# 384-token feed-forward steps, a 32x32 convolution and a new instruction order in a fused linear-attention and gated-feed-forward kernel

## The chip, the cores and the metric

The kernel runs on one core of a Trainium2 chip. The metric is the device time of one execution in microseconds (us), lower is better: the median of three runs. A profile of one execution stands beside it. Its span is a little shorter than the time of the run that it belongs to.

Five engines work side by side, each in the order of its own instructions: TensorE (PE), VectorE (DVE), ScalarE (ACT), GpSimd (POOL) and SyncE (SP), which here only issues transfers. Matrix products land in PSUM, in banks; all else lies in SBUF.

## The reference

A linear attention with a decaying state feeds a gated feed-forward block. B = 4 batches, H = 8 heads, S = 768 tokens, D = 48, all float32; H*D = 384 channels.

```python
def _attn_ref(r, k, v, w, u):
    for t in range(S):
        cur = einsum('bhd,bhe->bhde', u[None] * kt, vt)
        y[:, :, t] = einsum('bhd,bhde->bhe', rt, state + cur)
        state = w[None, :, :, None] * state + einsum('bhd,bhe->bhde', kt, vt)

def _moe_ref(x, w_val, conv_w, w_out):            # x: y as [B, S, 384]
    xp = np.concatenate([zeros((B, K - 1, D)), x], axis=1)     # K = 5 taps, causal
    for k in range(K):
        gate_pre += conv_w[k][None, None, :] * xp[:, k:k + S, :]
    gate = 1.0 / (1.0 + np.exp(-gate_pre))
    return gate * (x @ w_val) @ w_out
```

## The kernel before

The attention works in 12 units n of 256 tokens (three to a batch), each of two chunks cl of 128. The order of all instructions is a long list of short names (ORDER), which the kernel walks; every engine gets its instructions in the order in which their names stand. The names that matter here: `r`, `k`, `v` loads; `RS`, `KS` scaling of r and k by powers of the decay; `RT`, `KT` their transposes on PE, `RE`, `KE` the copies of these out of PSUM; `PR`, `S`, `SE`, `DV` the bonus of the current token; `CV` the cast of v; `A`, `M` scores and their mask; `KV`, `ID`, `ZE` the state; `YD`, `Y`, `YE` the output of the attention, written to `xT` (channels on partitions, tokens along the row); `C` convolution, `SG` sigmoid, `V` values, `HT` gate times value, `O` projection, `OE` its copy, `st` the store. A star moves the step to another engine or queue.

```python
    ld = ctx.enter_context(tc.tile_pool(name="ld", bufs=7))        # k and v
    ldr = ctx.enter_context(tc.tile_pool(name="ldr", bufs=6))      # r
    outp = ctx.enter_context(tc.tile_pool(name="outp", bufs=11))   # outputs
    psum = ctx.enter_context(tc.tile_pool(name="psum", bufs=8, space=bass.MemoryType.PSUM))

    def load_kv(n, cl, nm, eng):          # 192 KB, rows of 48 floats
        eng.dma_start(out=d[n][:, cl], in_=src[b, :, t0 : t0 + C, :].transpose([1, 0, 2]))

    def carry(n, cl):                     # ID: add the carried state
        kv_ps = st["kv_ps", n, cl]
        nc.vector.tensor_tensor(out=kv_ps, in0=kv_ps, in1=st["zin", n, cl], op=ALU.add)

    def evac_k(n, cl=None):               # KE
                nc.scalar.copy(out=st["kT", n].rearrange(...)[:, cls[0] : cls[1]], in_=tr)
```

The feed-forward works on 256 tokens at a time. The five taps are products with 64x64 diagonal matrices (`cwd`). 384 channels are three groups of 128; the third group is laid beside the first two, so that each of two banks holds 256 + 128 columns:

```python
    def conv(n):
        g_ps = [bank([128, W + C]) for i in range(2)]          # W = 256, C = 128
        for T0, t1, tn in ((0, 0, W), (2, 0, 0)):
            for t in range(KW):
                for q in range(2):
                    for i in range(2):
                        T = 2 if T0 else i
                        c0, n0, o0 = (i * C, C, W) if T0 else (t1, tn, t1)
                        rows = slice(64 * q, 64 * q + 64)
                        qo = (q + i) % 2
                        nc.tensor.matmul(
                            out=g_ps[i][64 * qo : 64 * qo + 64, o0 : o0 + n0],
                            lhsT=cwd[rows, T, t, :],
                            rhs=xT[rows, T, t0 + c0 + t : t0 + c0 + t + n0],
                            ...)
    # values: three matmuls of 256 and three of 128 columns for each of two halves
    # projection: three matmuls of 384 columns for each chunk of 128 tokens
    # the last unit is done chunk by chunk in functions of its own (conv_l, value_l, project_l ...)
    def store(n):                          # one row of 384 floats (1536 B) after the other
        nc.sync.dma_start(
            out=out[b, cu * W : cu * W + W, :].rearrange("(c p) n -> p c n", p=128),
            in_=st["o", n])
```

In ORDER, all stores stand behind the last load on the queue of SP.

Of the kernel before, what the change touches and what calls it, by code (L numbers as in the profile page):

```python
# [16 lines left out]
def kernel(  # L17
# [15 lines left out]
    C = 128  # L33
# [12 lines left out]
    ld = ctx.enter_context(tc.tile_pool(name="ld", bufs=7))  # L46
    ldr = ctx.enter_context(tc.tile_pool(name="ldr", bufs=6))
# [3 lines left out]
    outp = ctx.enter_context(tc.tile_pool(name="outp", bufs=11))  # L51
# [54 lines left out]
    io_i32 = consts.tile([128, 1], mybir.dt.int32)  # L106
    nc.gpsimd.iota(io_i32, pattern=[[0, 1]], base=0, channel_multiplier=1)
    io_j = consts.tile([128, 2], mybir.dt.int32)
    nc.gpsimd.iota(io_j, pattern=[[1, 2]], base=0, channel_multiplier=2)
    mask = consts.tile([128, 128], BF16)  # L110
    make_upper_triangular(nc, mask, val=1.0, diag=False)

    io_f = consts.tile([128, 1], F32)
    nc.vector.tensor_copy(io_f, io_i32)
    sc_k = consts.tile([128, U], F32)
    for cl in range(U):
        nc.vector.tensor_scalar(
            sc_k[:, cl : cl + 1], io_f, scalar1=-1.0, scalar2=float(C - 1 - cl * C),
            op0=ALU.mult, op1=ALU.add,
        )  # L120
    sc_r = consts.tile([128, 2], F32)
    nc.vector.tensor_copy(sc_r, io_j)
    nc.vector.tensor_scalar_add(sc_r, sc_r, float(-C))
# [76 lines left out]
    nc.gpsimd.memset(wcm, 0.0)  # L200
    bdm = consts.tile([128, NP, 2, D], F32)
    nc.gpsimd.memset(bdm, 0.0)
    for par in range(2):
        nc.gpsimd.memset(bdm[64 * par : 64 * par + 64, :, par, :], 1.0)
# [3 lines left out]
    wv_st = consts.tile([128, NT, DM], F32)  # L208
    wo_st = consts.tile([128, NT, DM], F32)

    wval = consts.tile([128, NT, 4, 128], BF16)
    wout = consts.tile([128, 4, DM], BF16)
    cw5b = consts.tile([KW, DM], BF16)
    cwT = consts.tile([128, NT, KW], F32)
    cwd = consts.tile([128, NT, KW, 64], BF16)
    id64 = consts.tile([128, 64], BF16)

    for q in range(2):
        rows = slice(64 * q, 64 * q + 64)
        nc.vector.tensor_copy(id64[rows], ident[rows, rows])  # L220
# [11 lines left out]
    def cw_evac():  # L232
        nc.vector.tensor_copy(cwT, st["cw_ps"][:, :, 0:KW])

    def cw_diag():
        nc.vector.tensor_tensor(
            out=cwd.rearrange("p t k x -> p (t k) x"),
            in0=id64[:, None, :].to_broadcast([128, NT * KW, 64]),
            in1=cwT.rearrange("p t k -> p (t k)")[:, :, None].to_broadcast([128, NT * KW, 64]),
            op=ALU.mult,  # L240
        )

    def cast_wval():
        wv = wv_st.rearrange("p k (t x) -> p k t x", x=128)
        nc.gpsimd.tensor_copy(wval[:, :, 0::2, :], wv[:, :, 0::2, :])
        nc.gpsimd.tensor_copy(wval[:, :, 1::2, 64:128], wv[:, :, 1:3, 0:64])
        nc.gpsimd.tensor_copy(wval[:, :, 1::2, 0:64], wv[:, :, 1:3, 64:128])

    def cast_wout(part):
        if part:  # L250
            nc.scalar.copy(out=wout[64:128, 1::2, :], in_=wo_st[0:64, 1:3, :])
            nc.scalar.copy(out=wout[0:64, 1::2, :], in_=wo_st[64:128, 1:3, :])
        else:
            nc.gpsimd.tensor_copy(wout[:, 0::2, :], wo_st[:, 0::2, :])


# [39 lines left out]
    def cast_v(n):  # L296
        vb = vb_t[n % 4]
        nc.scalar.copy(  # L298
            out=vb[:, :, 16 : 16 + 64 * H].rearrange("p c (h x) -> p c h x", x=64)[:, :, :, 0:D],
            in_=v_st[n],  # L300
        )
# [17 lines left out]
    def evac_k(n, cl=None):  # L319
        for cls, tr in st["tr", n]:  # L320
            if cl is None or cl == cls[0]:
                nc.scalar.copy(  # L322
                    out=st["kT", n].rearrange("x n (c i) -> x c n i", c=U)[:, cls[0] : cls[1]],
                    in_=tr,
                )
# [83 lines left out]
    def carry(n, cl):  # L409
        kv_ps = st["kv_ps", n, cl]  # L410
        nc.vector.tensor_tensor(out=kv_ps, in0=kv_ps, in1=st["zin", n, cl], op=ALU.add)
# [55 lines left out]
    def evac_y(n, cl):  # L467
        b, cu = divmod(n, NU)
        t0 = PAD + cu * W + cl * C
        nc.scalar.copy(out=xT_t[b % 2][:, :, t0 : t0 + C], in_=st["y_ps", n, cl])  # L470


    def conv(n):
        b, cu = divmod(n, NU)
        xT, t0 = xT_t[b % 2], cu * W
        g_ps = [bank([128, W + C]) for i in range(2)]
        for T0, t1, tn in ((0, 0, W), (2, 0, 0)):
            for t in range(KW):
                for q in range(2):
                    for i in range(2):  # L480
                        T = 2 if T0 else i
                        c0, n0, o0 = (i * C, C, W) if T0 else (t1, tn, t1)
                        rows = slice(64 * q, 64 * q + 64)
                        qo = (q + i) % 2
                        nc.tensor.matmul(  # L485
                            out=g_ps[i][64 * qo : 64 * qo + 64, o0 : o0 + n0],
                            lhsT=cwd[rows, T, t, :],
                            rhs=xT[rows, T, t0 + c0 + t : t0 + c0 + t + n0],
                            start=(t == 0 and T0 == 0 and t1 == 0),
                            stop=(t == KW - 1),  # L490
                            skip_group_check=True,
                        )
        st["g_ps", n] = g_ps

    def gate_at(n, i):
        if ("gate", n) not in st:
            st["gate", n] = ffn.tile([128, 2, W + C], BF16, name="gate")
        nc.scalar.activation(out=st["gate", n][:, i], in_=st["g_ps", n][i], func=AF.Sigmoid)  # L498

    def value(n, i):  # L500
        b, cu = divmod(n, NU)
        xT, t0 = xT_t[b % 2], PAD + cu * W
        v_ps = bank()[:, 0 : W + C]
        for kt in range(NT):
            nc.tensor.matmul(  # L505
                out=v_ps[:, 0:W],
                lhsT=wval[:, kt, i, :],
                rhs=xT[:, kt, t0 : t0 + W],
                start=(kt == 0),
                stop=(kt == NT - 1),  # L510
                skip_group_check=True,
            )
        for kt in range(NT):
            nc.tensor.matmul(  # L514
                out=v_ps[:, W : W + C],
                lhsT=wval[:, kt, 2 + i, :],
                rhs=xT[:, kt, t0 + i * C : t0 + i * C + C],
                start=False,
                stop=(kt == NT - 1),
                skip_group_check=True,  # L520
            )
        st["v_ps", n, i] = v_ps

    def gated(n, i):
        if ("hT", n) not in st:
            st["hT", n] = ffn.tile([128, 2, W + C], BF16, name="hT")
        nc.vector.tensor_tensor(  # L527
            out=st["hT", n][:, i], in0=st["v_ps", n, i], in1=st["gate", n][:, i], op=ALU.mult
        )

    def project(n, cl):
        hT = st["hT", n]
        o_ps = bank()[:, 0:DM]
        parts = [(0, cl * C, 0), (1, cl * C, 1)]
        parts.insert(1 + cl, (cl, W, 2 + cl))
        for j, (i, c0, k) in enumerate(parts):
            nc.tensor.matmul(  # L537
                out=o_ps,
                lhsT=hT[:, i, c0 : c0 + C],
                rhs=wout[:, k, :],  # L540
                start=(j == 0),
                stop=(j == 2),
            )
        st["o_ps", n, cl] = o_ps

    def evac_o(n, cl):
        if ("o", n) not in st:
            st["o", n] = outp.tile([128, U, DM], F32, name="o_sb")
        nc.scalar.copy(out=st["o", n][:, cl, :], in_=st["o_ps", n, cl])  # L549

    def store(n):
        b, cu = divmod(n, NU)
        nc.sync.dma_start(
            out=out[b, cu * W : cu * W + W, :].rearrange("(c p) n -> p c n", p=128),
            in_=st["o", n],
        )

    HC = C // 2  # L560
    WL = C + HC

    def conv_l(n, cl):
        b, cu = divmod(n, NU)
        xT, t0 = xT_t[b % 2], cu * W + cl * C
        g_ps = [bank()[:, 0:WL] for i in range(2)]
        for T0 in (0, 2):
            for t in range(KW):
                for q in range(2):
                    for i in range(2):  # L570
                        T = 2 if T0 else i
                        c0, n0, o0 = (i * HC, HC, C) if T0 else (0, C, 0)
                        rows = slice(64 * q, 64 * q + 64)
                        qo = (q + i) % 2
                        nc.tensor.matmul(
                            out=g_ps[i][64 * qo : 64 * qo + 64, o0 : o0 + n0],
                            lhsT=cwd[rows, T, t, :],
# [254 lines left out]
```

## Time and profile before

| what | value |
|---|---|
| time, median of 3 (range) | 104.25 us (103.94 to 104.44) |
| span of the profiled run (its time) | 101.9 us (103.68) |
| PE, DVE, ACT, POOL busy | 84.5, 73.5, 72.7, 66.1 us |
| moved | 20.37 MB in 67505 packets, mean 200 GB/s |
| of these under 512 B | 63510 |
| convolution matmuls | 440, and 80 in the last unit |
| scores: DVE mask | 48 of 681 ns, 30.9 us |

How to read it. A busy time is the sum of an engine's instructions. Matmuls overlap one another, so PE's busy time counts latencies, and the cost of a block of matmuls is taken from the timeline or from the chain of waits, where a piece has a start and a length. The chain of waits follows the last instruction back to what released it, again and again; a piece "DMA v_st" is a load that something waited for, "SPq" is the issue of a transfer. A row of a group reads: line, engine, operation, what is written from what, shapes, count, then busy us and mean ns, then idle time ahead of it and what ended it. Windows give the busy time of each engine in a stretch of the span.

### The profile page before, as it was taken

What the parts mean: (1) busy time and instruction counts of PE and PEld (TensorE: products, weight loads), DVE (VectorE), ACT (ScalarE), POOL (GpSimd) and SP (SyncE); (2) the same over time, 40 slices, a digit from 0 to 9 for tenths busy, and PEclk for the clock granted to TensorE, in tenths of its full rate; (3) what the DMA queues carried; (4) which work ended last, traced back from release to release, by engine and by line L of the source; (5) the groups of instructions that cost most, each with busy time, mean ns of one, the idle gap of its engine ahead of it and who ended that gap; (6) DMA issues with size and microseconds to landing.
All of it is one profiled execution on the core that took longest, in us unless ns stands there. A gap on an engine that the chain in (4) does not pass through costs nothing.

```text
span 101.9 us, 4626 instructions
## 1 busy us (share of the span) xinstructions
PE 84.5 (83%) x2017; PEld 69.4 (68%) x2017; DVE 73.5 (72%) x145; ACT 72.7 (71%) x126; POOL 66.1 (65%) x67
## 2 busy tenths in 40 slices
PE   1413987998969799989999999988999999999900
PEld 1202766876858587978887887876888788778500
DVE  4057798999765685889989998489678898980500
ACT  5457574999294998887988939688979868538510
POOL 7928678969499884999775686798692571400000
PEclk9999999999999999999999999999999999999985
DMA  0999999999989998999999999798989894750660
GB/s 7 253 220 168 234 175 192 270 244 171 277 165 249 203 216 180 200 185 250 173 191 223 187 248 222 142 204 187 185 162 251 306 363 145 271 198 7 250 218 5
DMA packets 67505, 20.37 MB, mean 200 GB/s; under 512 B 63510, under 2 KB 67484, under 8 KB 67484
## 3 DMA queue, kind: packets, MB, share of 16 engines
q1 hardware_dynamic: 64428, 19.18, 85.0%
q10 hardware_dynamic: 3056, 0.89, 4.0%
q8 instruction: 16, 0.26, 1.1%
q14 instruction: 5, 0.04, 0.1%
HBM read 15.35 MB, written 4.72 MB: 197 GB/s over the span
## 4 chain that ended last, share of the span: by engine, by line
PE 28%; SPq 24%; DMA 18%; POOL 12%; ACT 8%; issue 5%; POOLq 0%
SPq L69 19%; DMA v_st<-in_v_dram 15%; POOL dv L358 7%; PE bank L537 6%; PE bank L485 5%; PE bank L441 4%; POOL ks L289 4%; SPq L76 4%; DMA r_st<-in_r_dram 3%; ACT xT L470 2%; PE bank L505 2%; PE bank L427 2%; ACT kT L322 2%; PE bank L399 1%; ACT rT L282 1%
## 5 line engine op out<-in xcount | busy, mean ns | idle before, releaser
L385 DVE TENSOR_TENSOR at<-bank,mask 128x512 bf16<-128x512 f32 x48 | 30.9, 681 | 3.4 <-PE bank L372 3.3
L260 POOL TENSOR_TENSOR rs<-r_st,dr 128x768 bf16<-128x768 f32 x11 | 20.0, 1821 | 7.5 <-DMA r_st<-in_r_dram 7.5
L289 POOL TENSOR_TENSOR ks<-k_st,dk 128x768 bf16<-128x768 f32 x10 | 18.2, 1822 | 8.1 <-DMA k_st<-in_k_dram 4.4
L358 POOL TENSOR_TENSOR dv<-v_st,s_sb 128x768 bf16<-128x768 f32 x12 | 17.7, 1476 | 4.4 <-DVE s_sb L355 2.9
L282 ACT COPY rT<-bank 128x1024 bf16<-128x1024 bf16 (+1 forms) x13 | 15.9, 1231 | 2.6 <-PE bank L274 2.6
L322 ACT COPY kT<-bank 128x1024 bf16<-128x1024 bf16 (+1 forms) x13 | 12.5, 959 | 4.7 <-DVE pr L331 1.7
L527 DVE TENSOR_TENSOR hT<-bank,gate 128x384 bf16<-128x384 f32 x22 | 11.8, 552 | 4.2 <-PE bank L514 2.5
L470 ACT CAST xT<-bank 128x384 bf16<-128x384 f32 x24 | 11.0, 493 | 3.5 <-PE bank L441 3.5
L537 PE MATMUL bank<-wout,hT 128*128 128x384 bf16 x66 | 13.4, 327 | 0.0
L298 ACT CAST vb<-v_st 128x768 bf16<-128x768 f32 x12 | 10.0, 836 | 4.1 <-DMA v_st<-in_v_dram 4.1
L485 PE MATMUL bank<-xT,cwd 64*64 64x128 bf16 (+1 forms) x440 | 11.5, 245 | 0.9 <-ACT xT L470 0.4
L498 ACT ACTIVATE gate<-bank 128x384 bf16<-128x384 f32 x22 | 10.0, 493 | 2.6 <-PE bank L485 2.4
L485 PEld LDWEIGHTS <-cwd 64*64 64x64 bf16 x440 | 9.9, 106 | 2.5 <-issue 1.5
L549 ACT COPY o_sb<-bank 128x384 f32<-128x384 f32 x22 | 10.7, 501 | 1.2 <-PE bank L537 1.2
L505 PE MATMUL bank<-xT,wval 128*128 128x256 bf16 x66 | 10.8, 273 | 0.1
L312 PE MATMUL bank<-ident,ks 128*128 128x128 bf16 x96 | 8.8, 242 | 1.8 <-DVE ks L289 1.8
L372 PE MATMUL bank<-rT,kT 48*128 48x128 bf16 x192 | 9.0, 232 | 1.0 <-ACT kT L322 0.7
L331 DVE TENSOR_TENSOR pr<-bank,rT 128x1024 bf16<-128x1024 bf16 (+1 forms) x13 | 8.4, 645 | 1.9 <-ACT kT L322 1.3
L274 PE MATMUL bank<-ident,rs 128*128 128x128 bf16 x96 | 8.6, 242 | 1.1 <-DVE rs L260 0.8
L441 PE MATMUL bank<-at,vb 128*32 128x128 bf16 x384 | 9.0, 219 | 0.0
L312 PEld LDWEIGHTS <-ks 128*128 128x128 bf16 x96 | 6.8, 109 | 2.5 <-POOL rs L260 2.0
L274 PEld LDWEIGHTS <-rs 128*128 128x128 bf16 x96 | 6.7, 109 | 1.9 <-issue 1.0
(80 smaller groups left out, 137.8 us busy)
## 6 DMA issues: line engine op xcount, KB each, us to landing
k_st<-in_k_dram SPq DMA_DIRECT2D x24, 192.0 KB, 5.5
v_st<-in_v_dram SPq DMA_DIRECT2D x24, 192.0 KB, 4.5
out_dram<-o_sb SPq DMA_DIRECT2D x11, 384.0 KB, 4.5
r_st<-in_r_dram SPq DMA_DIRECT2D x9, 384.0 KB, 5.6
r_st<-in_r_dram ACTq DMA_DIRECT2D x2, 384.0 KB, 5.1
wv_st<-in_moe_w_val_dram SPq DMA_DIRECT2D x1, 576.0 KB, 6.2
wo_st<-in_moe_w_out_dram SPq DMA_DIRECT2D x1, 576.0 KB, 6.0
r_st<-in_r_dram SPq DMA_DIRECT2D x2, 192.0 KB, 3.5
```

Source lines behind the costliest of these rows:

```text
L69: eng.dma_start(out=d[n][:, cl], in_=src[b, :, t0 : t0 + C, :].transpose([1, 0, 2]))
L260: eng.tensor_tensor(out=rs_t[n % 2][:, :, ps[0] : ps[1], :, 0:D].rearrange("p s n a d -> p (n a) s d"), in0=r_st[n][:, hs], in1=dr[:, hs], ...
L274: nc.tensor.transpose(tr[:, s, p, :], rs_t[n % 2][:, s, ps[0] + p].rearrange("p a x -> p (a x)"), ident,)
L282: nc.scalar.copy(out=st["rT", n][:, ps[0] : ps[1], :].rearrange("x n (i s) -> x s n i", s=2), in_=st["r_tr", n, ps[0]],)
L289: eng.tensor_tensor(out=ks_t[n % 3][:, cs, :, :, 0:D].rearrange("p c n a d -> p c (n a) d"), in0=k_st[n][:, cs], in1=dk[:, cs], op=ALU.mult,)
L312: nc.tensor.transpose(tr[:, c, p, :], ks[:, cls[0] + c, p].rearrange("p a x -> p (a x)"), ident,)
L322: nc.scalar.copy(out=st["kT", n].rearrange("x n (c i) -> x c n i", c=U)[:, cls[0] : cls[1]], in_=tr,)
L358: eng.tensor_tensor(out=dv_t[n % 2].rearrange("p c (h d) -> p (c h) d", d=D), in0=v_st[n].rearrange("p c h d -> p (c h) d"), in1=st["s", n ...
L385: nc.vector.tensor_tensor(out=st["at", n, cl][:, par], in0=st["at_ps", n, cl][par], in1=mask[:, None, :].to_broadcast([128, NP, 128]), op= ...
L441: nc.tensor.matmul(out=y_ps[32 * q : 32 * q + 32, T, :], lhsT=lt, rhs=rh, start=False, stop=last, skip_group_check=True,)
L485: nc.tensor.matmul(out=g_ps[i][64 * qo : 64 * qo + 64, o0 : o0 + n0], lhsT=cwd[rows, T, t, :], rhs=xT[rows, T, t0 + c0 + t : t0 + c0 + t + ...
L537: nc.tensor.matmul(out=o_ps, lhsT=hT[:, i, c0 : c0 + C], rhs=wout[:, k, :], start=(j == 0), stop=(j == 2),)
```

## The change

It changes the feed-forward and, around it, the order of everything.

- The feed-forward works in steps of 384 tokens (half a batch), the last half batch in steps of 256 and 128. There are nine steps. Each of the three channel groups has a bank of its own.
- The convolution uses 32x32 diagonal matrices: 12 matmuls for each tap, each in a tile of its own of the PE array. The 64-column diagonals shrink to 32 columns. The channels come out rotated by 32 for the second and 64 for the third group, so the columns of w_val and the rows of w_out are rotated too (w_out while it is loaded, in five pieces).
- The stores write three token rows one after the other from each partition.
- The carried state is added by PE, with an identity matrix.
- Some copies out of PSUM move from ACT to DVE, three casts of v to POOL, two scalings of r to DVE.
- Seven early loads have their issue on the queue of ACT, where there were two. Buffers for k and v are 9, for r 8, for outputs 6 (larger ones, shared with the staging of the two weights).
- Constants are made in fewer instructions; six dummy matmuls stand early in PE's order.
- ORDER is another one throughout, searched anew over 24 cases, with one reader at a time for each PSUM bank.

The computation is the same, apart from roundings.

```diff
-    ld = ctx.enter_context(tc.tile_pool(name="ld", bufs=7))
-    ldr = ctx.enter_context(tc.tile_pool(name="ldr", bufs=6))
+    ld = ctx.enter_context(tc.tile_pool(name="ld", bufs=9))
+    ldr = ctx.enter_context(tc.tile_pool(name="ldr", bufs=8))
-    outp = ctx.enter_context(tc.tile_pool(name="outp", bufs=11))
+    outp = ctx.enter_context(tc.tile_pool(name="outp", bufs=6))
 ... (constants, memsets of wcm and bdm from POOL to DVE)
-    cwd = consts.tile([128, NT, KW, 64], BF16)
+    cwd = consts.tile([128, NT, KW, 32], BF16)
 ...
     def carry(n, cl):
-        nc.vector.tensor_tensor(out=kv_ps, in0=kv_ps, in1=st["zin", n, cl], op=ALU.add)
+        nc.tensor.matmul(
+            out=st["kv_ps", n, cl].rearrange("p n a d -> p (n a d)"),
+            lhsT=ident, rhs=st["zin", n, cl].rearrange("p n a d -> p (n a d)"),
+            start=False, stop=True, skip_group_check=True)
 ...
+    def taps(g_ps, xT, t0, n0):
+        for t in range(KW):
+            for T in range(NT):
+                for b in range(4):
+                    rows, q = slice(32 * b, 32 * b + 32), 32 * ((b + T) % 4)
+                    nc.tensor.matmul(
+                        out=g_ps[T][q : q + 32, 0:n0],
+                        lhsT=cwd[rows, T, t, :],
+                        rhs=xT[rows, T, t0 + t : t0 + t + n0],
+                        start=(t == 0), stop=(t == KW - 1), skip_group_check=True)
+    STEPS = [(b, f, 3) for b in range(B - 1) for f in (0, 3)]
+    STEPS += [(B - 1, 0, 3), (B - 1, 3, 2), (B - 1, 5, 1)]
 ...
+    def value(m, T):            # three matmuls of n0 = 384, 256 or 128 columns
+    def project(m, j, half=None):
+            nc.tensor.matmul(
+                out=o_ps,
+                lhsT=st["hT", m][:, T, 0 : span(m)[2]].rearrange("p (i c) -> p c i", i=C)[:, j],
+                rhs=wout[:, T, c0 : c0 + n0], start=(T == 0), stop=(T == NT - 1))
     def store(m):
-            out=out[b, cu * W : cu * W + W, :].rearrange("(c p) n -> p c n", p=128),
+            out=out[b, t0 : t0 + n0, :].rearrange("(p c) n -> p (c n)", p=128),
 ... (the functions of the last unit go; the last 128 tokens are projected and stored in two halves)
-        w wt:0 r:0.0 WB:0 wt:1 r:0.1 cw r:1* CWB WB:1 LN:0 k:0.0 DRI:0 k:0.1 LN:1 ut:1 k:1.1 DKI:0
+        w k:1.0* ut:1 r:0.0 wt:1 r:0.1 r:1* WB:0 WB:1 cw k:1.1* wt:0 k:0.1 k:0.0 LN:0 LN:1 CWB
 ... (the rest of ORDER)
```

## The prediction

> **What bounds the kernel now.** I read the busy shares and slices on the page first, then the chain of waits in order of time, then busy time by stage, and last the groups of instructions. The page opens so:
>
> ```profile
> PE 84.5 (83%) x2017; PEld 69.4 (68%) x2017; DVE 73.5 (72%) x145; ACT 72.7 (71%) x126; POOL 66.1 (65%) x67
> ...
> DMA  0999999999989998999999999798989894750660
> ```
>
> No engine is full by this line, and four stand within 20 points of one another; but the transfer engines are at 0.9 or more from the second slice (2.5 us) to about 76 us. So a share over the whole run decides nothing. The chain of waits (start, length, what) tells two stages apart:
>
> ```profile
> 22.80 5.00 DMA v_st<-in_v_dram
> ...
> 49.66 4.22 DMA v_st<-in_v_dram
> ...
> 60.89 5.63 DMA v_st<-in_v_dram
> 66.52 0.03 POOLq L358
> ...
> 67.67 1.49 POOL dv L358
> 69.16 0.05 issue
> 69.21 0.51 PE bank L427 x6
> ...
> 78.96 0.88 ACT kT L322
> ...
> 96.74 0.22 PE bank L633 x2
> ```
>
> Up to 69.2 us the chain returns again and again to a load of v: the loads pace the kernel. From 69.2 to 97 us it stays on PE, with detours over ACT. Busy time by stage (columns PE, PEld, DVE, ACT, POOL, then clock, transfer share, GB/s) says the same:
>
> ```profile
> 45.90:69.20 23.30, 22.39 (x586) 18.74 (x584) 20.22 (x40) 18.93 (x33) 17.93 (x12) 1.00 1.04 206
> 69.20:97.00 27.80, 27.50 (x718) 22.16 (x718) 20.32 (x40) 20.38 (x41) 11.52 (x7) 1.00 0.72 211
> 97.00:101.90 4.90, 0.00 (x0) 0.00 (x0) 0.00 (x0) 0.30 (x1) 0.00 (x0) 0.66 0.32 102
> ```
>
> Stage one (to 69.2 us) has transfers at 1.04 of their time and 206 GB/s. Stage two has PE busy 27.5 of 27.8 us while transfers fall to 0.72. Stage three is a tail of 4.9 us: last copy and last store. In stage two the ACT pieces of the chain add up to 5.5 us (0.42 + 0.50 + 0.71 + 1.21 + 0.88 between 75.8 and 79.8, then 0.88 and 0.88), so PE and ACT together set it.
>
> The rows that the change touches:
>
> ```profile
> L485 PE MATMUL bank<-xT,cwd 64*64 64x256 bf16 x220 | 8.5, 273 | 0.9 <-ACT xT L470 0.4 <-DVE at L385 0.3
> L411 DVE TENSOR_TENSOR bank<-bank,z 128x384 f32<-128x384 f32 x8 | 4.5, 564 | 1.0 <-PE bank L399 0.7
> L322 ACT COPY kT<-bank 128x1024 bf16<-128x1024 bf16 x11 | 11.3, 1027 | 3.5 <-DVE pr L331 1.7 <-PE bank L537 1.4 <-PE bank L312 0.3
> L260 POOL TENSOR_TENSOR rs<-r_st,dr 128x768 bf16<-128x768 f32 x11 | 20.0, 1821 | 7.5 <-DMA r_st<-in_r_dram 7.5
> ```
>
> The mean of a matmul (273 ns) is a latency; its cost is read in the chain or timeline, where 40 convolution matmuls take 1.02 us, 0.95 us from their start to the next piece's.
>
> **What the Trainium skill says.** "TensorEngine Tiling (Array Packing)", section Available Configurations: the array can be 4 tiles of 64x64 or 16 of 32x32. "TensorE: Matmul & The Clock Gate", section Measured speedup vs the span model, gives 6.32x for 9 and 10.6x for 16 tiles of 32x32. The trace before has only four tiles of 64x64: 40 matmuls stream 20x256 + 20x128 = 7680 columns, 1920 per tile. Three full 384-column matmuls take 0.49 us, so a column costs 0.43 ns, 1920 cost 0.82 us, and 0.95 to 1.02 were taken: 81 to 86% of perfect packing. No run here yet shows 32x32. "DMA: Bandwidth & Descriptors", section Issuing engines are not separate DMA queues: transfers issued from two queues share 16 engines, and only issue time is saved. The trace agrees in that transfers are at 0.9 or more while one queue issues nearly all of them. "PSUM — Partial Sum Buffer", section PSUM bank collisions raise a hardware error, says that two engines on one bank at once are not stalled but an error, so software must order them; the wait of ACT for the DVE product on the same bank (kT for pr, 1.7 us) is such an order.
>
> **The change part by part.**
>
> Convolution. Before: 11 blocks of 0.97 us and a last one of 80 matmuls in 1.00 us, 11.7 us. After: 9 steps of 60 matmuls, 12 tiles in use. A 384-token step streams 60x384/12 = 1920 columns per tile, what a 256-token block streams now. At today's packing it is 0.97 us again, for half as many tokens more; 7 make 6.8. The steps of 256 and 128 tokens are limited by instruction rate (80 took 1.00 us, 12.5 ns each): 0.75 us each. Sum 8.3, a gain of 3.4. Between the skill's 9 and 16 tiles I read about 8x for 12: 60 x 165 ns / 8 = 1.24 us a step, sum some 10.2, a gain of 1.5. I take 2.7.
>
> Value and projection. Columns per token are the same. Values cost 0.50 us per half block: 11.0, plus 1.1 at the end; after, 81 matmuls of 165, 110 or 55 ns: 11.9. Gain 0.2. Projection: 66 x 0.164 plus 1.7 for the split last pieces, 12.5; after, 69 x 0.164 + 6 x 0.085 = 11.8. Gain 0.7.
>
> Carry. Eight additions of 564 ns leave DVE (4.5 us) and become eight identity matmuls of 384 columns, 0.165 us each, 1.3 us on PE. Six dummy matmuls of 512 columns (1.3 us) stand early, where PE waits for loads. PE's net relief: 2.7 + 0.2 + 0.7 - 1.3 = 2.3 us.
>
> ACT. Five kT copies (5.1 us), two of xT (1.0) and a net three of the output (1.5) go to DVE, three casts of v (2.5) to POOL; the cast of w_out is 0.5 shorter, the gates 0.2 longer. ACT falls from 72.7 to about 62.
>
> DVE. Minus 4.5 (carry), 0.9 (half the diagonal) and 1.5 (constants). Plus 5 kT copies at 0.69 or less (the product of the same shape takes 686 ns): 3.4; 5 copies of 384: 2.8; two scalings of r at about 0.96 (what one k of that shape took there, 958 ns): 1.9; gating in three sizes: 0.7; memsets: 1.3. Net +3, to about 77. POOL: minus two scalings of 1.82, a cast of 0.8 and memsets of 1.3, plus three casts of v at perhaps 0.9 (the w_out cast of as many elements took 822 ns) and small ones: about 64.
>
> Transfers. The same loads; stores become one run of 4608 B per partition instead of three of 1536. They run after the loads, when transfers are not full, so I count nothing but a possible 0.5 us at the end. Loads on ACT's queue: transfers are full from 2.5 us on, so at most the half-empty first slices can be gained, 0.5 us.
>
> Sum. Stage one is paced by loads and moves by 0.5 us. In stage two there lie four conv blocks and the last double one, 4.9 us, of which a quarter (2.7 of 11.7), 1.2, goes, and 0.7 of the projection; two carries add 0.3: 1.6 us. Of the 5.5 us of ACT detours I count half as gone, 2.7, as ACT loses a seventh of its work. Together -4.8; I give back 1.5 for what a new order makes late elsewhere (DVE is fuller, the first loads are shared by two blocks). The span goes from 101.9 to 98.6. The profiled run was 103.68 us for a span of 101.9, 1.8 more, and the median 104.25 is 2.3 more: I say 101.0, and round up to 101.3, as order is the part I cannot compute.
>
> **Rivals.** First, loads stay the bound: the same bytes at the same 206 GB/s end near 80 us, and if PE already waits on them, faster PE work only makes it wait. For it: the chain to 69 us. Against it: 17 us of PE work after the last load has landed, which the shorter convolution cuts. It would give 102.5 to 104. Second, DVE becomes the bound: 77 us plus waits, with kT copies that PE's score matmuls need. Against it: its 72% share leaves 28 us. It would give 103 to 105. Third, PSUM: a step now holds three banks for the gates and three for values out of eight, where a block held two; PE would wait for a free bank, seen as waits of PE on gate or hT. It would give 102 to 105. Fourth, the first block: ACT issues three large loads before its first logarithm, r and k of block 1 share the transfers with block 0, and everything starts 1 to 2 us later: 102 to 103. Fifth, 32x32 tiles that share rows don't run side by side: with only four at once a step would take 60 x 165 / 4 = 2.5 us and the convolution 19 or so, +7 us and 108. The 64x64 tiles share rows already and reach over 80%, so I give this little.
>
> **Range and chances.** Full success (convolution 8.3, all detours gone, head and stores 1 us) gives about 98.5; rivals one to four lie at 102 to 105. Range 98.4 to 104.6. Faster by over 2% means under 102.2: 0.60. Within 2%: 0.28. Slower, above 106.3, by a bad order or by the fifth rival: 0.12.
>
> **What will show it.** The convolution's pieces of 60 matmuls in the timeline: 0.95 to 1.25 us. ACT near 62 us, DVE near 77, the additions of the carry gone. The chain from about 69 us on still PE, with fewer ACT pieces. The last v landing within 1.5 us of 80. PE's last matmul near 93.5 instead of 97, and a tail of about 5 us. The prediction is wrong if the chain stays on loads of v to 80 us or later, if PE shows waits for banks in the middle, or if the first score matmuls start over 1 us after 12.2 us.

## The result and the profile after

The changed kernel takes **99.91 us**, the median of 4 runs (99.19 to 100.47). The kernel before took 104.34 in the runs beside them (4 runs, 103.94 to 105.04). The ratio is 0.956, with an interval of 0.948 to 0.965. The profiled run took 99.79 us with a span of 98.0 us, 3.9 below the 101.9 of before.

The page of the kernel after opens with the busy times; the second line is the transfers' row of the 40 slices:

```profile
PE 82.5 (84%) x1973; PEld 61.3 (63%) x1973; DVE 73.9 (75%) x147; ACT 64.7 (66%) x113; POOL 61.7 (63%) x70
...
DMA  1999999988969699979797998969997479602753
```

ACT has lost 8 us (72.7 to 64.7), PE 2, and DVE is where it was (73.5 to 73.9) although it took over copies. The transfers still stand near 0.9 to about 70 us.

Busy time by stage, kernel after (start and end, length, then PE, PEld, DVE, ACT, POOL, clock, transfer share, GB/s):

```profile
45.90:69.20 23.30, 21.67 (x508) 16.25 (x506) 20.03 (x39) 17.07 (x29) 18.59 (x13) 1.00 0.92 198
69.20:92.00 22.80, 22.56 (x650) 16.34 (x650) 17.66 (x35) 14.90 (x28) 10.44 (x7) 1.00 0.66 210
92.00:98.00 6.00, 2.40 (x39) 1.59 (x23) 1.66 (x5) 1.89 (x6) 0.00 (x0) 0.99 0.52 201
```

The stages are the old ones: a first in which transfers run at 0.92 and PE has gaps, a second in which PE is busy 22.56 of 22.80 us, and a tail. The chain of waits of the kernel after, at the passage between the first two and at its end (start, length, what):

```profile
63.83 4.42 DMA k_st<-in_k_dram
...
68.27 0.84 POOL rs L254
...
72.26 0.97 PE bank L483 x60
...
93.11 0.48 ACT o_sb L470
93.60 0.49 ACT o_sb L470
94.12 0.68 PE bank L540 x6
94.82 0.36 DVE o_h L468
```

Up to 68 us the chain still goes back to a load, now one of k. After that it is PE without a break until 93.1 us: the two output copies of 0.48 and 0.49 us are the only ACT pieces left, where before had 5.5 us of them. A piece of 60 convolution matmuls costs 0.97 us.

The span's 3.9 us lie in two places. PE's last matmul ends at 94.8 instead of 97.0 us: 2.2. The tail from there to the end is 3.2 instead of 4.9 us: 1.7.

Groups of the kernel after, shapes kept apart, for what the change put in (count, then busy us, mean ns, then idle time before):

```profile
L470 ACT COPY kT<-bank 128x1024 bf16<-128x1024 bf16 x6 | 6.1, 1014 | 2.7 <-DVE pr L324 2.2 <-PE bank L306 0.5
L468 DVE COPY kT<-bank 128x1024 bf16<-128x1024 bf16 x5 | 3.4, 685 | 0.2 <-PE bank L306 0.2
```

The same copy takes 685 ns on DVE and 1014 on ACT, so moving it is also a saving.

### The profile page after: what moved, and what is told of

Its sections match the earlier page's. It is cut to its first block, busy times and chain, and to the rows that moved or that the text cites. A ratio compares the mean times of both kernels' runs of the same rounds, so it can differ in the third digit from the quotient of the medians.

```text
span 98.0 us, 4531 instructions
## 1 busy us (share of the span) xinstructions
PE 82.5 (84%) x1973; PEld 61.3 (63%) x1973; DVE 73.9 (75%) x147; ACT 64.7 (66%) x113; POOL 61.7 (63%) x70
## 3 DMA queue, kind: packets, MB, share of 16 engines
q1 hardware_dynamic: 58348, 18.59, 77.9%
## 4 chain that ended last, share of the span: by engine, by line
PE 44%; SPq 31%; DMA 13%; DVE 3%; POOL 2%; issue 2%; ACT 1%; POOLq 0%
SPq L69 18%; DMA k_st<-in_k_dram 9%; PE bank L540 8%; PE bank L516 7%; PE bank L440 7%; SPq L242 7%; PE bank L483 5%; SPq L76 5%; PE bank L365 4%; DMA r_st<-in_r_dram 4%; PE bank L268 3%; PE bank L306 3%; DVE at L378 2%; PE bank L392 2%; PE bank L426 2%
## 5 line engine op out<-in xcount | busy, mean ns | idle before, releaser
L254 POOL TENSOR_TENSOR rs<-r_st,dr 128x768 bf16<-128x768 f32 x9 | 16.5, 1830 | 0.2 <-POOL ks L283 0.2
L528 DVE TENSOR_TENSOR hT<-bank,gate 128x384 bf16<-128x384 f32 (+2 forms) x27 | 13.3, 508 | 3.6 <-PE bank L516 2.6
L516 PE MATMUL bank<-xT,wval 128*128 128x384 bf16 (+2 forms) x81 | 15.1, 308 | 0.0
L540 PE MATMUL bank<-wout,hT 128*128 128x384 bf16 (+1 forms) x75 | 14.4, 321 | 0.4 <-ACT o_sb L470 0.4
L508 ACT ACTIVATE gate<-bank 128x384 bf16<-128x384 f32 (+2 forms) x27 | 10.7, 459 | 4.1 <-PE bank L483 3.9
L292 ACT CAST vb<-v_st 128x768 bf16<-128x768 f32 x9 | 7.6, 840 | 2.9 <-DMA v_st<-in_v_dram 2.9
L483 PE MATMUL bank<-xT,cwd 32*32 32x384 bf16 (+2 forms) x540 | 9.3, 317 | 0.0
L516 PEld LDWEIGHTS <-wval 128*128 128x128 bf16 x81 | 6.9, 98 | 3.5 <-issue 0.2
L470 ACT COPY kT<-bank 128x1024 bf16<-128x1024 bf16 (+1 forms) x8 | 7.2, 915 | 2.7 <-DVE pr L324 2.2
L540 PEld LDWEIGHTS <-hT 128*128 128x128 bf16 x75 | 6.7, 103 | 3.6 <-DVE hT L528 0.6
```

What stands on the lines that cost most here:

```text
L254: eng.tensor_tensor(out=rs_t[n % 2][:, :, ps[0] : ps[1], :, 0:D].rearrange("p s n a d -> p (n a) s d"), in0=r_st[n][:, hs], in1=dr[:, hs], ...
L470: nc.scalar.copy(out=out, in_=in_)
L483: nc.tensor.matmul(out=g_ps[T][q : q + 32, 0:n0], lhsT=cwd[rows, T, t, :], rhs=xT[rows, T, t0 + t : t0 + t + n0], start=(t == 0), stop=(t ...
L516: nc.tensor.matmul(out=v_ps, lhsT=wval[:, kt, T, :], rhs=xT_t[b % 2][:, kt, PAD + t0 : PAD + t0 + n0], start=(kt == 0), stop=(kt == NT - 1),)
L540: nc.tensor.matmul(out=o_ps, lhsT=st["hT", m][:, T, 0 : span(m)[2]].rearrange("p (i c) -> p c i", i=C)[:, j], rhs=wout[:, T, c0 : c0 + n0] ...
```

## The experiments

Three theories were put to the test.

- **Relief.** PE's path got shorter: 12 tiles make the convolution cheaper, and the copies that left ACT no longer stand between PE's pieces.
- **Loads.** The early loads on ACT's queue, or deeper buffers, bring the data sooner, and the rest follows.
- **Order.** The new order makes the gain, and the single moves matter little.

The kernels called a_ are the changed kernel with one edit, those called b_ the kernel before with one edit. Each ratio is against the kernel before on the same chip, with a 95% interval. Medians and ranges are of all runs of a kernel, while ratios leave out the runs in a slower state that every kernel falls into at times (a_actmore and b_run384 have one other run each, and so no ratio).

### The changed kernel once more (a_again), and its stores in short runs (a_store3)

a_again has no edit. a_store3 has the token order and the 1536 B runs of the old stores:

```diff
-                lhsT=st["hT", m][:, T, 0 : span(m)[2]].rearrange("p (i c) -> p c i", i=C)[:, j],
+                lhsT=st["hT", m][:, T, j * C : j * C + C],
-            out=out[b, t0 : t0 + n0, :].rearrange("(p c) n -> p (c n)", p=128),
+            out=out[b, t0 : t0 + n0, :].rearrange("(c p) n -> p c n", p=128),
```

> The changed kernel once more, beside the others on one chip: 99.9 us, within 0.5. All theories agree.

> The changed kernel with stores in three runs of 1536 B per partition and the projection from contiguous columns. If the 4608 B runs are why the tail after PE's last matmul fell from 4.9 to 3.2 us, 1.0 to 1.7 us come back (101 to 101.6) and PE's last matmul stays near 94.8. If the tail is shorter because less is left to store at the end, the time stays within 0.4 of the changed kernel.

a_again took 98.72 us (6 runs, 98.29 to 100.96), ratio 0.950 (0.942 to 0.959). Its profiled execution has PE's last matmul at 93.5 us and a tail of 3.2. The shares of its chain are PE 72% and queue of SP 5%; the first profile had PE 44% and queue of SP 31%. So the shares of the chain are a property of one execution, and are not compared between kernels here.

a_store3 took 100.16 us (97.95 to 101.06), ratio 0.947 (0.931 to 0.963), and its tail is 3.3 us. Its interval holds the ratio of a_again: the length of the stores' runs buys nothing measurable, and is not what shortened the tail.

### Copies back on ACT (a_act), and the same relief in the old order (b_relief)

a_act gives the ten copies out of PSUM and the three casts of v back to ACT, by taking the star from their entries in ORDER (KE, OE, YE, CV), and leaves all else. b_relief is the reverse: in the old kernel, with its old order, ten such copies go to DVE and three casts to POOL.

```diff
 a_act
-        KEP:0.0 RS:2 KT:1 KE:1* D:1 ...
+        KEP:0.0 RS:2 KT:1 KE:1 D:1 ...        (and twelve more)
 b_relief
-                nc.scalar.copy(out=st["kT", n]..., in_=tr)
+                copy(vec, st["kT", n]..., tr)   # DVE where starred: KE 1,3,5,8,11; YE 9.0,11.0;
+                                                # OE 2.0,4.1,6.0; casts 3,6,9 on POOL
```

> The changed kernel with all ten PSUM copies that went to DVE, and the three casts of v that went to POOL, back on ACT, same order. If the ACT detours of stage two (5.5 us on the chain before, about 1 now) went because ACT was relieved, 1.5 to 3 us come back (101.4 to 103). If they went because of the new order, ACT has over 30 us idle and the time stays within 0.5.

> The kernel before with the relief of ACT alone: five copies of kT, two of xT and three of the output on DVE, three casts of v on POOL, in its old order. Undoing the relief in the changed kernel cost 3 to 4 us. If it is worth the same by itself: 101 to 102.5 us. If it only pays within an order made for it: within 1 us of 104.6, or slower, as DVE now has the carry too.

a_act took 102.66 us (22 runs, 101.13 to 103.57), ratio 0.978 (0.974 to 0.983). Against the 0.950 of a_again on the same chip that is 2.8% of about 104 us, some 3 us more. ACT is busy 72.8 us, as in the kernel before. Its chain of waits has pieces of ACT again, all of them between 45.9 and 72.5 us, such as these:

```profile
55.34 0.72 ACT vb L292
56.06 0.38 ACT o_sb L470
56.44 0.93 ACT kT L470
57.37 0.05 issue
57.41 0.40 PE bank L365 x8
```

A cast of v, an output copy and a kT copy, one after the other on ACT, and then the score matmuls that need that kT. None of the three work on the same data: they are serial because they share a queue.

Busy time by stage, first of a_again and then of a_act (columns as above, PE first):

```profile
20.40:45.90 25.50, 24.36 (x608) 18.47 (x616) 20.61 (x40) 18.37 (x31) 22.49 (x18) 0.87 0.96 211
45.90:69.20 23.30, 23.30 (x584) 17.84 (x564) 21.35 (x41) 18.51 (x31) 20.70 (x14) 1.00 0.93 201
```

```profile
20.40:45.90 25.50, 21.36 (x490) 15.48 (x490) 18.32 (x35) 17.95 (x28) 19.61 (x16) 0.93 0.95 211
45.90:69.20 23.30, 22.66 (x632) 17.32 (x630) 18.12 (x35) 20.35 (x34) 18.77 (x12) 1.00 0.92 196
```

From 20.4 to 69.2 us PE stands still for 4.8 us in a_act and for 1.1 us in a_again. After that there is no such difference (0.2 and 0.1 us from 69.2 to 92 us). So what the relief saves lies in stage one, not in stage two, where the expectation looked for it. Of the 4.8 us, 3.0 are one wait at 31.6 us, behind DVE and a late load of r; how much of that wait comes from the moves is not separated.

b_relief took **108.89 us** (108.08 to 109.31), ratio 1.048 (1.041 to 1.055): the same moves make the old kernel slower, although ACT fell to 65.0 us there too, and although its tail is shorter (below). The waits of b_relief say how (engine and line, what for, us in total, times, longest):

```profile
ACT o_sb L323 <- PE bank L542: 7.3, 4, 3.3
...
PE bank L404 <- POOL vb L298: 3.4, 2, 2.1
...
DVE hT L532 <- ACT o_sb L323: 3.1, 1, 3.1
```

PE waits up to 2.1 us for a cast of v on POOL, and DVE up to 3.1 us for a copy on ACT. Each engine takes its instructions in order; a copy that was early enough in ACT's queue is late in the place where DVE or POOL comes to it. So the theory of relief falls in its plain form. What the two runs show together is that relief and order are one change: with an order made for it, the relief is worth about 3 us, and in the old order it costs 5. What the order would bring without the moves is not separated by any run, nor is what the deeper buffers bring.

### The carry on DVE again (a_carry_dve)

```diff
-        nc.tensor.matmul(out=..., lhsT=ident, rhs=..., start=False, stop=True, skip_group_check=True)
+        nc.vector.tensor_tensor(out=kv_ps, in0=kv_ps, in1=st["zin", n, cl], op=ALU.add)
```

> The changed kernel with the carried state added by DVE again (8 times 564 ns on DVE, 8 times 0.16 us less on PE). If PE alone sets stage two: equal or up to 0.5 us faster. If DVE's latency in the chain of the state matters: 0.5 to 1.5 us slower.

It took 100.56 us (6 runs, 99.27 to 102.80), ratio 0.965 (0.950 to 0.981). The median is 1.8 us above that of a_again, but the intervals of the two ratios overlap: not separated. DVE's busy time rises to 77.0 us.

### Four tiles of 64x64 (a_conv64) and 32x32 tiles in another order (a_taps4)

a_conv64 keeps steps of 384 tokens and goes back to 64-wide diagonals: 30 matmuls a step, rotation by 64 for the odd channel group. a_taps4 keeps the 32x32 tiles and turns the two outer loops, so that the five taps of one channel group follow one another.

```diff
 a_conv64
-    cwd = consts.tile([128, NT, KW, 32], BF16)
+    cwd = consts.tile([128, NT, KW, 64], BF16)
-                for b in range(4):
-                    rows, q = slice(32 * b, 32 * b + 32), 32 * ((b + T) % 4)
+                for b in range(2):
+                    rows, q = slice(64 * b, 64 * b + 64), 64 * ((b + T) % 2)
 a_taps4
-        for t in range(KW):
-            for T in range(NT):
+        for T in range(NT):
+            for t in range(KW):
```

> The changed kernel with the convolution in 64x64 tiles (30 matmuls a step, four tiles in flight, 2880 columns per tile in a step of 384). Each of seven steps should take 1.46 us instead of 0.97, in all some 4 us more PE work, of which four steps lie after 60 us. If PE work in stage two sets the end: 1.5 to 2.5 us slower (101.4 to 102.4). If loads set the end and PE has slack: under 0.7 us slower.

> The changed kernel with the loop over channel groups outside the loop over taps: the same 60 matmuls a step, but only four different tiles in a row. If twelve tiles in flight are what makes a step 0.97 us, it becomes 60 x 165 / 4 = 2.5 us, PE gets some 12 us more in all, and the time rises by 5 to 10 us. If tiles overlap by instruction count whatever their order, the step stays near 1 us and so does the time.

The chain of waits of a_conv64, and after it that of a_taps4, for one step of 384 tokens (the kernel after has 0.97; two of the 60 records are missing from the second piece):

```profile
72.81 1.75 PE bank L486 x30
```

```profile
76.36 1.62 PE bank L483 x58
```

a_conv64 took 101.73 us (4 runs, 100.77 to 104.54), ratio 0.973 (0.961 to 0.986). 1.75 us is explained by its tiles: groups 0 and 2 have the same rotation, so two of the four tiles get 10 matmuls of 384 columns, 3840 columns at 0.43 ns, 1.65 us. With steps of 256 and 128 tokens (1.21 and 0.68 for 0.76 and 0.63) the convolution costs PE 6.0 us more than in the kernel after.

a_taps4 took 103.46 us (102.50 to 105.18), ratio 0.984 (0.972 to 0.997). Counted at full clock, seven steps at about 1.62 and the two small ones at 1.21 and 0.77 make 5.1 us more on PE. The same 540 matmuls, in the same tiles, in another order, give back more than half of the change's gain.

So PE time of the convolution does count, but not in full. Against the two runs of the kernel after (0.950 and 0.956 of about 104.5), a_conv64 loses 1.8 to 2.4 us of its 6.0, with its interval overlapping that of the second, and a_taps4 2.9 to 3.6 of its 5.1, with intervals apart. A microsecond of convolution is worth between three and seven tenths of a microsecond here.

### Loads: their queue (a_spq, b_actq, a_actmore) and their speed (a_run384, b_run384)

a_spq puts the early large loads of r, k and v that the changed kernel issues from ACT back on SP. They are six, not the seven of the list of changes, and the kernel before had one of them there (the four of w and u stay, which both kernels had on ACT). b_actq moves five early loads of the kernel before to ACT. a_actmore moves, in the changed kernel, four more loads of r and five of v to ACT in mid-run. All are stars in ORDER:

```diff
 a_spq
-        w k:1.0* ut:1 r:0.0 wt:1 r:0.1 r:1* WB:0 WB:1 cw k:1.1* ...
+        w k:1.0 ut:1 r:0.0 wt:1 r:0.1 r:1 WB:0 WB:1 cw k:1.1 ...   (k:2.1, v:1.0, v:1.1 too)
 b_actq
+        k:1.1* k:1.0* k:2.1* v:1.1* v:1.0*
 a_actmore
+        r:6* r:7* r:8* r:9* v:4.1* v:5.1* v:6.1* v:7.1* v:8.1*
```

> The changed kernel with its six large early loads issued on SP's queue again, in the same places of the order. The new theory is that two queues move more than one: in the traces so far, 260 GB/s against 195 between 5 and 10 us, and loads that end at 77.2 us instead of 80.1. If so, some 0.4 MB less will have been loaded by 10 us, the last load lands 1.5 to 3 us later, and the time rises by 1.5 to 3 us. If the order or the buffers brought the loads forward, both stay within 0.7.

> The kernel before with five more early loads (k of units 1 and 2, v of unit 1) on ACT's queue, in the same places of its order. Two-queue theory: the last load lands 1 to 3 us earlier than 80.1 and the time falls by 1 to 2.5 us. If PE and ACT alone set the end, the time stays within 0.7 or rises as ACT is held up early.

> The changed kernel with nine more loads on ACT's queue in mid-run: r of units 6 to 9 and the second half of v of units 4 to 8. If a second queue moves more at any time, loads end 1 to 3 us earlier than 77 and the time falls by 1 to 2 us. If 16 engines are full in mid-run, or ACT issues too late in its own order, the loads end no earlier and the time stays or rises by up to 2 us.

The windows from 5 to 10 us, of the kernel before, of the kernel after and of a_spq (the last three columns are clock, transfer share and GB/s):

```profile
5.00:10.00 5.00, 1.25 (x11) 0.93 (x11) 3.00 (x4) 3.18 (x9) 2.78 (x5) 1.00 1.28 195
```

```profile
5.00:10.00 5.00, 1.20 (x11) 0.90 (x12) 2.76 (x6) 3.67 (x9) 0.56 (x3) 1.00 1.24 260
```

```profile
5.00:10.00 5.00, 1.53 (x15) 1.24 (x16) 3.01 (x6) 2.89 (x8) 2.09 (x4) 1.00 1.12 248
```

The changed kernel moves a third more in these 5 us than the kernel before, at the same share. Putting the loads back on SP makes 248 GB/s of 260, and 123 of 147 in the 5 us ahead: 1.90 MB are moved by 10 us instead of 2.08. The other variants with these loads on ACT (a_run384 apart) have 145 to 151 GB/s in the first 5 us and 251 to 262 in the next, so only the first difference is clear. The last load lands at 79.8 instead of 77.2 us, but also anywhere from 76.8 to 80.0 us in the variants that have the same loads on ACT. The time of a_spq is 100.19 us (4 runs, 99.53 to 101.81), ratio 0.961 (0.953 to 0.969), not separated from the kernel after. The early loads do come sooner by ACT's queue, and little or nothing of it reaches the end.

b_actq took 105.69 us (105.30 to 106.07), ratio 1.016 (1.010 to 1.022). The loads gained nothing that lasted (195 became 214 GB/s from 5 to 10 us, but 204 became 190 from 10 to 15, and the last landed at 80.8 for 80.1), and PE's timeline in b_actq shows the first score matmuls at 16.95 us, where before had them at 12.20. What they wait for stands in the chain of waits of b_actq:

```profile
6.60 7.32 DMA k_st<-in_k_dram
...
13.94 0.37 ACTq L69
...
14.36 1.32 ACTq L69
...
15.72 0.73 ACT rT L282
16.45 0.94 ACT kT L322 x2
```

A load of k comes late, and then two issues of v on ACT's own queue (0.37 and 1.32 us) keep it from the copies of rT and kT that the scores need.

a_actmore took 104.54 us (4 runs, 101.80 to 105.14). Its last load lands at 73.8 us, 3.4 sooner than in the kernel after, and yet each of its runs is slower than each of that. Its nine issues take 0.37 to 1.75 us each of ACT's queue, 5.1 us in all. The timelines of a_actmore, one of the longest issue and one of PE soon after it (the bracket is PE's idle time before, and what ended it):

```profile
41.70 1.75 ACTq L69 DMA_DIRECT2D v_st<-in_v_dram  x1
```

```profile
42.20 0.33 PE L392 MATMUL bank<-vb,ks 128*128 128x96 bf16 x4 [0.95 <-ACT vb L292]
...
45.99 0.65 PE L540 MATMUL bank<-wout,hT 128*128 128x384 bf16 x3 [1.37 <-ACT rT L276]
```

a_again has neither of these two idle times of PE. So loads that arrive sooner in exchange for ACT's time are a bad trade. That alone would say that loads don't pace the kernel. The last two runs say otherwise: they load k and v in runs of 384 B instead of 192 B, by taking two neighbouring tokens to a partition. That permutes tokens and heads inside a load, so these two kernels compute an output that isn't the reference's; the amount of work is the same.

```diff
-        t0 = cu * W + cl * C
-        eng.dma_start(out=d[n][:, cl], in_=src[b, :, t0 : t0 + C, :].transpose([1, 0, 2]))
+        hs = slice(H // 2 * cl, H // 2 * cl + H // 2)
+        eng.dma_start(
+            out=d[n][:, cl].rearrange("p (h s) d -> p h (s d)", s=2),
+            in_=src[b, hs, cu * W : cu * W + W, :].rearrange("h (p s) d -> p h (s d)", s=2))
```

> The changed kernel with k and v loaded in runs of 384 B as r is, instead of 192 B: the same bytes in half the packets, heads and tokens permuted, so the output is not the reference's. Transfers should need about 13 us less in all (24 loads of each at 1.63 us for a pair instead of 2.2). If loads pace the first 69 us, the time falls by 3 to 6 us (94 to 97). If PE and its partners set the pace all along, by under 1 us.

> The kernel before with the same wider runs in its loads of k and v (output permuted too). If loads pace it as the chain says, 2 to 5 us faster than 104.3. The difference to the changed kernel with the same loads is then what the change brings where loads pace nothing: about its PE relief and ACT detours, 4 to 6 us, if PE sets the end; only 1 to 2 us if the change worked through the loads.

a_run384 took 95.71 us (4 runs, 94.82 to 96.05), ratio 0.916 (0.905 to 0.927), with the last load at 61.6 us. b_run384 took 100.14 (4 runs, 98.27 to 100.75), with the last load at 66.1. Against the ratios of the changed kernel (0.950 and 0.956) the 0.916 of a_run384 means 3.5 to 4.2 us for loads that are faster at no cost to an engine. In the kernel before they bring 4.5 us between the medians (104.64 in the runs beside it). The change is worth 4.4 us between the medians beside fast loads, as it is with the ordinary ones (104.34 - 99.91), but only 2.6 us if the one run of b_run384 at 98.27 is taken, the only one fit for a ratio. So the gain of the change is not hidden by the loads, and at least half of it stays when they are faster. Whether the two add up in full stays open.

Where the loads pace differs between the kernels. In b_run384 the lead over the kernel before grows: its third, sixth and eighth convolution blocks start 1.0, 1.6 and 2.6 us sooner. In the changed kernel it is all there at the first convolution step, as the timelines of a_again and of a_run384 show:

```profile
26.89 1.49 PE L483 MATMUL bank<-xT,cwd 32*32 32x384 bf16 x60
```

```profile
23.13 1.04 PE L486 MATMUL bank<-xT,cwd 32*32 32x384 bf16 x60
```

From these starts to PE's last matmul it is 66.6 us in a_again and 67.9 in a_run384. Part of the 3.8 us between the starts goes with PE's clock, not with the loads directly: in a_run384 it was not lowered in this stretch (last section). In a_again PE is busy 23.30 of 23.30 us from 45.9 to 69.2 us, so no load holds it there; in the first trace of the kernel after, one does at 63.8 us.

### The tail

No run was made for the tail alone, but several differ in it. The transfer rows of the kernel before, of the kernel after and of b_relief for their last half store (KB, then us from issue to landing):

```profile
out_dram<-o_l ACTq DMA_DIRECT2D x1, 96.0 KB, 3.5
```

```profile
out_dram<-o_h ACTq DMA_DIRECT2D x1, 96.0 KB, 1.7
```

```profile
out_dram<-o_l ACTq DMA_DIRECT2D x1, 96.0 KB, 1.7
```

Same bytes, same 768 B packets; b_relief has the store code of the kernel before, and still lands in 1.7 us. What differs is in the packet records of the queues that the page calls "instruction". In the kernel before, a 16 KB packet (1.44 us) and an 8 KB packet (0.41 us) of these begin 2.3 and 2.1 us ahead of the last store's packet. From then on the stores' packets thin out: in the last 1.5 us before they end at 100.4 us, only 19 are left and run about one at a time, at 14 GB/s or less. That fits one engine of 16 holding all that is left, though the records used here don't name the engine. In the kernel after, the last such packets begin 4.4 and 2.6 us ahead and are over 2.3 us ahead of it, and from 95.0 to 96.5 us the transfers run at 0.95 to 1.03 until all is done. All fourteen traces sort the same way: the last half store lands in 1.7 to 1.9 us where no such packet begins in the 2.5 us ahead of the stores' last packet (the changed kernel with all its variants, and b_relief), and in 2.6 to 3.5 us where one does (before, b_actq, b_run384). From the end of the last copy to the end of the span that makes 4.6 us before, and 2.8 both after and in b_relief. So the tail's gain of 1.7 us is best read, though not shown, as where the program's own instruction transfers happen to fall. Nobody moved them on purpose, and no run moved them alone.

## Why the prediction was right, and where its steps were not

The predicted 101.3 us is 1.4 above the measured 99.91, inside the range, and the kernel is faster by over 2%, which had the largest chance. That the sum came so close is in part luck. The span was said to be 98.6 us and is 98.0, but PE's last matmul came 1.3 us later than said (94.8 for 93.5) and the tail was 1.8 us shorter. The other 0.8 of the 1.4 us is the step from the span to the time, taken as 2.7 us and measured as 1.9. And the largest term of the gain, ACT's detours, was sought in the wrong stage. Point by point:

**The convolution was mis-sized, low.** The step is "I take 2.7". Start to next piece, a step of 384 tokens took 0.97 us (five of the seven in a_again; one took 1.04, and the first, at a lowered clock, 1.42), the last two 0.76 and 0.63. With seven at 0.97 that is 8.2 us, for 11.7 before, so 3.5. The first estimate, that a step streams 1920 columns per tile as a block did before, gave 8.3 and was right to 0.1. The other came from the Trainium skill, "TensorE: Matmul & The Clock Gate", section Measured speedup vs the span model, by reading between 9 and 16 tiles. It gave 1.24 us a step; 60 x 165 ns in 0.97 us is 10.2x with 12 tiles, which that table gives for about 16. The measurement decides. Where a trace has the packing of the same kernel (0.82 us streamed, 0.95 taken), it was the better guide.

**ACT's detours were misread.** The step is "I count half as gone, 2.7". The 5.5 us stand on the chain of waits, and on the chain after 69 us they did shrink to 1.0 us. But a piece of the chain is not idle time of PE. Most of the detours lie here, in the kernel before:

```profile
75.00:80.00 5.00, 4.89 (x66) 4.08 (x67) 3.74 (x8) 4.34 (x8) 2.17 (x2) 1.00 0.90 225
```

PE worked 4.89 of these 5.00 us, on other blocks, and 27.50 of the 27.80 us of stage two. So the detours could give back 0.3 us there at most, not 2.7. The relief is worth about 3 us all the same (a_act), but before 69 us, where PE otherwise stands still. ACT's busy time fell to 64.7, not 62.

**Where the gain should show.** Stage one was to move by 0.5 us and stage two to bring the rest. The last convolution of the second batch ends at 56.74 us before and at 54.96 after, that of the third at 74.98 and 73.23, PE's last matmul at 97.0 and 94.8. So 1.8 of PE's 2.2 us were there by 55 us. In a_again it is 0.9 by the second batch, 2.9 by the third and 3.5 at the end. Most of the gain lies where the prediction expected next to none.

PE's last matmul was predicted near 93.5 and ended at 94.8 in one execution and 93.5 in the other. Of what the 1.5 us given back "for what a new order makes late elsewhere" stand for, two parts can be seen: PE stands still for 1.4 us at 19.3 us, until a cast of v, and soon after its clock is half for 3.5 us, 1.7 us by an estimate (last section). What the order alone costs was not measured.

**The tail** was predicted at 5 us, with a possible 0.5 for longer runs of the stores. It came out at 3.2, and a_store3 shows that the runs have no part in it. This step failed: the number of one profile was taken as fixed. b_relief, with the old stores, has a tail of 3.2 us too; that the rest was a meeting of transfers is the likely reading.

**The loads.** "Stage one is paced by loads" holds for the kernel before (b_run384). For the changed kernel it holds up to about 20 us (a_again), and after that only in the first of its two traces. A last landing within 1.5 us of 80 was off in the first trace (77.2 us). "At most 0.5 us" for the head cannot be judged: the time of a_spq is not separated. The Trainium skill, "DMA: Bandwidth & Descriptors", section Issuing engines are not separate DMA queues, says that starting transfers from several engines saves only the time of issuing them, and that this is usually small. For the transfers of the first 5 us it was not small (147 for 123 GB/s, after against a_spq); for the time of the kernel no difference is shown. The prediction took a transfer share near 1 for a full pipe; 195 GB/s at 1.28 and 260 at 1.24 show that it isn't a measure of that.

**The rivals.** The first, loads as the bound that hides the gain, would have given 102.5 us or more and did not come: PE's last matmul moved with the change, and beside fast loads the change is worth no more than with the ordinary ones. The second, DVE: 73.9 us instead of the feared 77, no bound. The third, PSUM: the only wait of PE for a bank's reader is 0.39 us at 93.7 us, for an output copy. The fourth, a later first block: its sign was seen, the first scores 1.8 us late (13.99 for 12.20), without its result, as they then ran faster: those of two units are done at 17.13 us for 16.96 (last section). The fifth, tiles that do not run side by side: a step of 0.97 us says they do.

## What to carry to other kernels

Moving work to an engine with room is half a change: the other half is the order in which the engines take it. Thirteen moves of the same kinds were worth about 3 us in an order made for them and cost 5 us in the old one. A detour on the chain of waits is no measure of the gain: 5.5 us of them on ACT went with 0.3 us of idle time of PE. Matmuls in small tiles want an order in which neighbours lie in different tiles: turning two loops made a convolution step 1.62 us instead of 0.97. And look into a tail before taking its length as given.

## What the runs showed that was not expected

**Matmuls overtake, it seems.** In a_taps4 strict issue in order would start a burst of 4 matmuls every 0.165 us, as the next tap needs the same four tiles: 15 bursts, 2.5 us. The starts in the trace fall into nine bursts of 4, 8, 8, 8, 12, 8, 4, 4 and 4, and the step takes 1.62 us. The simplest reading is that matmuls of the next channel group start beside those of the group ahead. Which record belongs to which matmul was not resolved, so the reading stays a reading.

**Twelve tiles at once.** In the kernel after a step is five bursts of 12 starts, each burst within 36 to 57 ns, 0.16 us apart: one 384-column stream after another, with all 12 tiles in use.

**The clock at the start.** The 16 score matmuls of a unit, in the kernel before and in the kernel after:

```profile
15.93 1.03 PE L372 MATMUL bank<-rT,kT 48*128 48x128 bf16 x16 [0.67 <-ACT kT L322]
```

```profile
13.99 0.62 PE L365 MATMUL bank<-rT,kT 48*128 48x128 bf16 x16
```

In the kernel before they take 306 ns in the mean from 12 to 20 us, and 219 ns from 21 us on. The trace's record of a full clock begins at 20.0 us there and at 12.6 us in the kernel after. In all ten traces of the changed kernel and its variants it begins at 11.9 to 14.5 us, in the four of the kernel before and its variants at 20.0 to 25.8. (The clock column of the windows says 1.00 earlier too, as there is no record.) The six dummy matmuls, which the prediction took as filling idle time only, stand in the ten kernels and not in the four. No run takes them out, so that they are the cause is not shown.

**A lowered clock near a pause.** PE stands still for 1.4 us until 20.8 us in the kernel after, and then this follows, with the granted clock as third from last:

```profile
22.80:26.30 3.50, 3.50 (x89) 2.66 (x96) 2.94 (x6) 2.49 (x4) 3.50 (x3) 0.51 1.05 273
```

Most of the first convolution step lies in it, which took 1.44 us instead of 1.04 by its own records. Half of 3.5 us, 1.7 us, is an estimate of what this cost; in a_again the stretch is 6.8 us long, and 3.4 us by the same estimate. The kernel before has none between 20 and 98 us. Eight of the ten traces with the new order have one or two such stretches of 3.4 to 6.8 us, each beginning within 2.1 us of the end of a pause of 0.95 to 3.5 us. The two without (a_conv64 and a_run384) have no pause over 0.6 us between 14 and 30 us. But pauses of 1.2 us at 64.8 us in the kernel after and of 2.2 us at 77.9 us in b_relief were followed by a full clock. So a pause alone does not decide it, and the cause was not tested.
